# Padded k and q loads, zero-tile fillers, three more low parts over TensorE, and unpaced expert weight loads

## The chip, the cores and the metric

The kernel runs on one core of one Trainium2 chip. The metric is device time in microseconds. Five engines run their own instruction queues in order: TensorE (matmuls), VectorE, ScalarE, GpSimd (POOL) and SyncE (SP, which here only issues loads). Data moves by 16 DMA engines. Profiles call VectorE DVE and ScalarE ACT; PEld is TensorE's weight load.

## The reference

Three stages are computed one after the other, on 4 sequences of 768 tokens with 8 heads of 48:

```python
# 1. gated linear attention, per head
state = alpha[t][:, None] * state + outer(k[t], v[t]);  y[t] = q[t] @ state
# 2. a dense layer, x: (3072, 384)
h = x @ w_in                                 # (384, 2048)
x = maximum(0.01 * h, h) @ w_out             # (2048, 384)
# 3. eight experts, each token to its best one
e = argmax(x @ w_gate); p = softmax(x @ w_gate)[e]
out = p * (maximum(x @ w1[e], 0) @ w2[e])    # w1[e]: (384, 1024), w2[e]: (1024, 384)
```

The dense layer's w_in and w_out arrive as 64-bit floats. The kernel takes their bits apart on VectorE and represents each scaled weight by two float16 parts, a high one (hi) and what is left (lo); products are summed as hi*hi + hi*lo + lo*hi.

## The kernel before, in words

Tokens are worked on in eight units of 384 (`NU`, `UT`). For each unit, alpha, k, q and v are loaded, VectorE forms running decays from alpha by a scan (L584), ScalarE their logarithms and inverses (L587, L589), and four VectorE products (L624) scale k and q by them into kt and qt. TensorE then transposes kt (L647), forms scores (L718), states and outputs (L679, L752, L759) in three chunks of 128 tokens, and the outputs are scaled (xh, L772), transposed and split into two float16 parts (L780 to L794). That is xT, the input of the dense layer, `moe1` (first half L830, second half L839; the leaky step in between is L807 to L814 on ScalarE, VectorE and POOL). After a unit, `finish` and `route` choose each token's expert and scatter its row to a table in HBM (L974).

Ahead of and beside the first unit the dense weights are unpacked. `w_in_piece` handles w_in in 12 pieces of 128 x 512: three VectorE passes over the bits (L421, L423, L425), the high part on ScalarE (L444), and then the low part in one of two ways: for pieces 0 to 5 two TensorE products that subtract the high part (L451, L452) and a ScalarE cast (L454), for pieces 6 to 11 one VectorE pass (L447). `w_out_piece` does the same bit passes for 16 pieces; `logit_weights` transposes each (L484), copies it out of PSUM scaled on ScalarE or VectorE, whichever the planner finds free (L488, L490), and multiplies it with w_gate (L495).

k and q come as two loads of 48 partitions each, into partitions 0 to 47 and 64 to 111 of a tile whose other partitions were set to zero once (L317 on POOL, L319 on ScalarE).

The order of all engines' queues is written by a planner, `Loom`, when the program is built. It keeps a clock for each engine, takes the chain of steps that could start first, and among those that could start within 0.25 us of it the one with the lowest priority number. A step names its cost (`O("A", 0.65)`), the events it needs and posts, and the ring buffers it takes. Load steps (`"D"`) have costs of their own, and a posted event of a load counts as landed some microseconds later. Where the planner sees TensorE idle for more than 0.5 us in the first two units, it puts filler matmuls there (`keep_warm`, L396), as many as the gap divided by 0.24; their operand is the float16 identity, made by POOL (L322).

The third stage runs over 26 tiles of 128 places in the table, in four phases of 256 columns of the experts' inner dimension. `first_weights` loads and splits phase 0's weights in 16 loads of 384 KB (`first_piece`: squares on ScalarE L357, the high part on ScalarE or VectorE, the low part on VectorE L1189), while the dense layer still runs, three buffers in a ring. When they and the dense layer's first half are done, the second phase's 16 loads may begin (`second_weights`); what is left of them is spread over the tiles of phase 0. Each tile stages its expert's weights two tiles ahead (`stage`, L1257), and TensorE does L1340 (first product) and L1369 (second). The rows of a tile are gathered (L1204) and transposed (L1218) some tiles ahead. `last_tiles` carries the last unit's routing and the second part of the table in between.

## Time and profile before

| | us |
|---|---|
| median of 3 runs | 785.34 (784.45 to 787.21) |
| the profiled execution | 784.73 |
| its span | 783.0 |
| TensorE busy | 748.6 (96%) |
| VectorE busy | 611.0 (78%) |
| ScalarE busy | 483.4 (62%) |
| POOL busy | 374.4 (48%) |

The span is what the profile covers; the execution's own time is 1.7 us more. Busy is the time in which an instruction of the engine runs; a matmul's end is modelled, so TensorE's share is not its share of peak. In rows of the timeline an `xN` is N instructions merged, and the bracket at the end is the idle time before the first of them and what ended it. [...]

### The profile page before, as it was taken

Reading aid. Unit: us, or ns where it says so; the run is one execution under the profiler, and the core shown is the slowest. Engines: PE = TensorE matmul, PEld = TensorE weight load, DVE = VectorE, ACT = ScalarE, POOL = GpSimd, SP = SyncE. Lnnn points to the kernel's source line nnn. Section 1 sums busy time; section 2 is a strip of 40 time slices with the busy share of each in tenths; the row PEclk is TensorE's granted clock in tenths of the full one; section 3 lists DMA queues with packets and bytes.
Section 4 is the critical chain, followed back from the end, with each engine's and each line's share of the span. In section 5 each row is a group of like instructions: output and inputs, shape, how many; then the busy total and the mean of one; then the engine's idle time right before and its main releaser. Section 6 shows DMA issues by size and latency. Waiting matters only on the chain.

```text
span 783.0 us, 20274 instructions
## 1 busy us (share of the span) xinstructions
PE 748.6 (96%) x7554; PEld 513.6 (66%) x7554; DVE 611.0 (78%) x1442; ACT 483.4 (62%) x1080; POOL 374.4 (48%) x406
## 2 busy tenths in 40 slices
PE   6989998999999999999999999998989999999994
PEld 2746665666566666766766665656877777777773
DVE  7899998489879868967965466574878899999664
ACT  5667654689976765774675382545666666667530
POOL 9126114523563272463373062363452487886543
PEclk9999999999999999999999999999999999999998
DMA  9663541154534535523001203115378565654342
GB/s 288 209 181 102 183 104 54 55 127 132 152 107 125 146 92 129 139 58 101 3 11 42 82 32 117 48 42 171 112 258 269 163 203 148 218 164 143 127 166 79
DMA packets 52872, 99.47 MB, mean 127 GB/s; under 512 B 5149, under 2 KB 37971, under 8 KB 52768
## 3 DMA queue, kind: packets, MB, share of 16 engines
q1 hardware_dynamic: 39104, 70.89, 31.8%
q0 software_dynamic: 4960, 14.62, 5.4%
q10 hardware_dynamic: 8704, 12.58, 4.6%
q8 instruction: 64, 1.05, 0.6%
q14 instruction: 40, 0.33, 0.1%
HBM read 76.03 MB, written 9.86 MB: 110 GB/s over the span
## 4 chain that ended last, share of the span: by engine, by line
PE 74%; DMA 7%; DVE 6%; POOL 5%; issue 4%; ACT 3%; DVEq 0%; ACTq 0%; POOLq 0%; SPq 0%
PE m L830 22%; PE m L839 20%; PE a L1340 9%; PE m L1369 9%; DMA wr<-in_moe_w 4%; PE a L718 3%; PE m L396 2%; POOL W L1140 2%; PE a L759 2%; PE a L679 1%; PE a L746 1%; PE a L647 1%; DMA so<-W 1%; DMA al<-in_aT 1%; PE a L495 1%
## 5 line engine op out<-in xcount | busy, mean ns | idle before, releaser
L839 PE MATMUL m<-woh,gh 128*128 128x392 f16 x1152 | 201.9, 330 | 0.0
L830 PE MATMUL m<-xT,wih 128*128 128x384 f16 x1152 | 194.0, 326 | 4.0 <-ACT xT L791 1.7
L814 POOL TENSOR_TENSOR gh<-gf,gh 128x384 f16<-128x384 f32 x128 | 118.8, 939 | 159.3 <-ACT gh L812 155.5
L830 PEld LDWEIGHTS <-wih 128*128 128x128 f16 x1152 | 111.4, 98 | 77.3 <-issue 4.7
L839 PEld LDWEIGHTS <-gh 128*128 128x128 f16 x1152 | 110.1, 98 | 73.4 <-issue 0.4
L1340 PE MATMUL a<-XT,st 128*128 128x128 f16 (+1 forms) x1872 | 116.8, 215 | 4.8 <-DVE st L1257 2.6
L1369 PE MATMUL m<-W,hs 128*128 (+1 forms) x624 | 119.3, 327 | 2.2 <-issue 1.6
L1340 PEld LDWEIGHTS <-st 128*128 128x128 f16 x1872 | 105.8, 98 | 22.6 <-DVE st L1257 4.7
L809 DVE SCALAR_TENSOR_TENSOR gf<-m,gf 128x384 f32<-128x384 f32 x128 | 70.2, 555 | 64.0 <-ACT gf L807 62.9
L1257 DVE COPY st<-W 128x1536 f16 x104 | 89.7, 863 | 22.2 <-PE m L1369 11.8
L807 ACT ACTIVATE gf<-m 128x384 f32<-128x384 f32 x128 | 62.4, 489 | 53.1 <-PE m L830 51.5
L1348 ACT ACTIVATE hs<-a 128x256 f16<-128x256 f32 x104 | 39.5, 381 | 68.1 <-PE a L1340 43.7
L1369 PEld LDWEIGHTS <-hs 128*128 128x128 f16 (+1 forms) x720 | 57.6, 101 | 31.9 <-issue 3.7
L812 ACT CAST gh<-gf 128x384 f16<-128x384 f32 x128 | 64.3, 506 | 11.3 <-DVE gf L809 11.2
L1140 POOL TENSOR_TENSOR W<-wr,W 128x768 f16<-128x768 f32 x32 | 56.8, 1777 | 4.5 <-ACT W L1139 4.4
L1204 POOL DMA_INDIRECT acc<-x_rows,offj x26 | 31.2, 1198 | 37.5 <-DVE offj L1201 31.2
L1352 DVE SCALAR_TENSOR_TENSOR hs<-a,hs 128x256 f16<-128x256 f32 x104 | 43.1, 414 | 7.2 <-ACT hs L1348 4.9
L1113 POOL TENSOR_SCALAR wr<-wr 128x768 f32<-128x768 f32 x32 | 29.8, 931 | 31.0 <-DMA wr<-in_moe_w 16.6
L357 ACT ACTIVATE scrap<-W 128x768 bf16<-128x768 f16 x48 | 40.2, 838 | 5.6 <-ACT hs L1348 3.9
L1390 POOL DMA_INDIRECT out<-acc x26 | 26.6, 1023 | 31.9 <-DVE acc L1387 20.9
L885 DVE TENSOR_REDUCE mx<-m 128x1 f32<-128x384 f32 x24 | 13.3, 553 | 33.8 <-PE m L839 28.9
L974 POOL DMA_INDIRECT x_rows<-xg,pi x24 | 25.0, 1041 | 23.0 <-PE m L830 5.2
(282 smaller groups left out, 1253.1 us busy)
## 6 DMA issues: line engine op xcount, KB each, us to landing
wr<-in_moe_w SPq DMA_DIRECT2D x64, 384.0 KB
so<-W ACTq DMA_DIRECT2D x32, 384.0 KB
al<-in_aT SPq DMA_DIRECT2D x16, 390.0 KB
raw_in<-in_moe_w_in SPq DMA_DIRECT2D x12, 512.0 KB
raw<-in_moe_w_out SPq DMA_DIRECT2D x16, 384.0 KB
ck<-in_moe_w_in SPq DMA_DIRECT2D x24, 256.0 KB
ck<-in_moe_w_out SPq DMA_DIRECT2D x32, 192.0 KB
kn__125<-in_kT SPq DMA_DIRECT2D x16, 288.0 KB
```

The costliest lines, as they stand in the source:

```text
L357: A.activation(scrap, src, AF.Square, scale=scale, accum_out=g_sq[:, i : i + 1])
L807: A.activation(gf, ph[:, 0:UT], AF.Copy, scale=0.01 * CG)
L809: V.scalar_tensor_tensor(gf, ph[:, 0:UT], CG, gf, ALU.mult, ALU.max)
L812: A.copy(gh[:, 0], gf)
L814: E_[e].tensor_tensor(out=gh[:, 1], in0=gf, in1=gh[:, 0], op=ALU.subtract)
L830: T.matmul(ph[:, 0:UT], wih[:, a, kk, f * P : (f + 1) * P], xT[:, b, kk, :], start=(n == 0), stop=(n == 8),)
L839: T.matmul(po[:, 0:ROW], g[f][:, a, c * P : (c + 1) * P], woh_[0][:, b, f, :], start=(n == 0), stop=(n == 3 * NF - 1),)
L1140: G.tensor_tensor(out=lo, in0=raw, in1=hi, op=ALU.subtract)
L1257: V.tensor_copy(out=sth[i % 2].rearrange("p a k f -> p a (k f)"), in_=Wp[ph][0][:, :, ds(reg(V, j), 1), :, :].rearrange("p a e k f -> p a ...
L1340: T.matmul(hp[:, f * P + z * w : f * P + (z + 1) * w], st[z][:, a, kk, f * P : (f + 1) * P], XT[j][:, b, kk, z * w : (z + 1) * w], start=( ...
L1352: V.scalar_tensor_tensor(hs[:, 1].rearrange("p i t -> p (i t)"), hp[:, 0 : 2 * P], 0.0, hs[:, 0].rearrange("p i t -> p (i t)"), ALU.max, A ...
L1369: T.matmul(yp[z * w : (z + 1) * w, 0:DM], hs[:, a, i, z * w : (z + 1) * w], w2, start=(n == 0), stop=(n == 5), skip_group_check=True,)
```

## The change

Five edits.

1. The fillers multiply a 128 x 128 float16 tile `idle` that VectorE sets to zero as its first instruction, instead of the identity. Their count is now (gap - 0.5)/0.25, and (gap - 2.0)/0.25 for the first gap.
2. The host pads k and q with zero rows to 64 per head, and one load of 128 partitions brings each; the tiles' zeroing goes. Their priority among the first unit's loads rises above that of the second w_in load. The planner's cost of loads in the first 20 us changes.
3. The low parts of w_in pieces 6, 7 and 8 go by TensorE and ScalarE as those of 0 to 5 do.
4. The scaled transposes of w_out are always copied by ScalarE.
5. The loads of the experts' first weights follow one another from issue to issue, not from landing to issue; pieces 11 to 15 get priority 1.5 instead of 20. The first two stages need the table only, and the last unit's three scatters go out in one step of `last_tiles`.

```diff
@@ Loom.do
-                self.warm(int((gap - 0.5) / 0.24))
+                self.warm(int((gap - (0.5 if self.clock["P"] else 2.0)) / 0.25))
...
-            t += us * (0.75 if e == "D" and t < DSTART else 1)
+            t += us * ((0.6 if t < 20 else 0.75) if e == "D" and t < DSTART else 1)
...
-        landed = t + op.lag + ((2.0 if t < DSTART else 4.0) if last == "D" else 0.0)
+        landed = t + op.lag + ((2.6 if t < 20 else 2.0 if t < DSTART else 4.0) if last == "D" else 0.0)
@@ tile_kernel
-    zero = cp.tile([P, 1], F32, name="zero")
-    V.memset(zero, 0.0)
+    idle = cp.tile([P, P], F16, name="idle")
+    V.memset(idle, 0.0)
...
-        t = pa.tile([P, 4, UT], F32, name=nm)
-        for p in (32, 96):
-            if nm == "kn_":
-                G.memset(t[p : p + 32], 0.0)
-            else:
-                A.copy(t[p : p + 32].rearrange("p a t -> p (a t)"), zero[p : p + 32].to_broadcast([32, 4 * UT]))
-        qk.append(t)
+        qk.append(pa.tile([P, 4, UT], F32, name=nm))
@@ keep_warm
-                    to.rearrange("p (a t) -> p a t", a=4), ident16,
-                    ident16.unsqueeze(1).to_broadcast([P, 4, P]), start=True, stop=True,
+                    to.rearrange("p (a t) -> p a t", a=4), idle,
+                    idle.unsqueeze(1).to_broadcast([P, 4, P]), start=True, stop=True,
@@ w_in_piece
-        if n >= 6:
+        if n >= 9:
@@ logit_weights
-        e = yield O("A", 0.5, take=[("wt", f)], free=[("a", ("wt", f))], alt=("V", (0.5,)))
+        yield O("A", 0.5, take=[("wt", f)], free=[("a", ("wt", f))])
...
@@ load_k
-        yield O("D", 2.6, take=[(nm, u, 2)], post=[(nm, u)])
-        for z in range(2):
-            nc.sync.dma_start(out=t[64 * z : 64 * z + D].rearrange("p a t -> p (a t)"), in_=src[u, z])
+        yield O("D", 3.1, take=[(nm, u, 2)], post=[(nm, u)])
+        nc.sync.dma_start(out=t.rearrange("p a t -> p (a t)"), in_=src[u])
@@ route
-            elif c:
-                yield
@@ first_weights
-            loom.add(first_piece(n, e, which), 20, now=loom.clock["V"])
+            loom.add(first_piece(n, e, which), 20 if n < 11 else 1.5, now=loom.clock["V"])
@@ first_piece
-        yield O("D", 1.8, take=[("wr", n)], need=[("wd", n - 1)] if n else (), post=[("wd", n)])
+        yield O("D", 1.8, take=[("wr", n)], need=[("wd", n - 1)] if n else ())
         raw = raw_weights(0, e, which)
+        loom.ev["wd", n] = loom.clock["D"], "D"
@@ first_stages
-            yield O("v", 0.75, need=[("wr", n) for n in range(E)] + [("acc", i)])
+            yield O("v", 0.75, need=[("wr", n) for n in range(E)] + ["table"])
@@ the units' loads
-            loom.add(load_k(u, nm, src, t), at - 0.7 * early)
+            loom.add(load_k(u, nm, src, t), at - 0.99 * early)
@@ last_tiles
         for _ in second_table():
-            next(work, None)
             yield
@@ _laid_out
+    def padded(a):
+        return np.pad(turned(a), ((0, 0), (0, 0), (0, 64 - D), (0, 0))).reshape(NU, P, H // 2 * UT)
...
-        "qT": turned(q),
-        "kT": turned(k),
+        "qT": padded(q),
+        "kT": padded(k),
```

## Rows read from the trace of the kernel before

**Rows 1.** Windows: start:end, length, five engines' busy us, PEclk, DMA share, GB/s.

```profile
0.00:21.00 21.00, 14.96 (x59) 6.40 (x60) 14.70 (x25) 10.00 (x15) 19.21 (x51) 1.00 0.91 279
21.00:40.00 19.00, 19.00 (x268) 13.90 (x267) 16.23 (x41) 13.44 (x28) 1.03 (x2) 1.00 0.67 218
21.00:54.00 33.00, 30.12 (x328) 19.82 (x327) 29.96 (x66) 21.88 (x44) 2.04 (x3) 1.00 0.74 225
54.00:100.00 46.00, 45.76 (x394) 29.13 (x394) 42.71 (x78) 31.63 (x84) 19.96 (x27) 1.00 0.42 130
100.00:136.00 36.00, 30.58 (x373) 22.18 (x373) 33.41 (x92) 18.66 (x46) 9.32 (x13) 0.95 0.30 69
136.00:517.00 381.00, 378.67 (x3213) 245.28 (x3211) 276.46 (x698) 253.63 (x591) 173.77 (x189) 1.00 0.32 89
517.00:545.00 28.00, 27.78 (x215) 17.87 (x214) 16.48 (x52) 11.58 (x20) 11.03 (x12) 1.00 0.36 107
570.00:606.00 36.00, 32.33 (x471) 25.41 (x469) 28.72 (x58) 25.25 (x42) 15.02 (x11) 1.00 0.87 282
```

**Rows 2.** TensorE's waits over the span: in total, times, longest.

```profile
PE m L396 <- POOL ident L322: 6.0, 1, 6.0
```

**Rows 3.** Timeline of the start and one later wait: start, length, instructions.

```profile
0.88 0.06 DVE L305 MEMSET zero<- 128x1 f32 x1 [0.88 <-PEq L1781]
6.04 15.06 PE L396 MATMUL m<-ident 128*128 128x512 f16 x58 [6.04 <-POOL ident L322]
11.01 9.60 PEld L396 LDWEIGHTS <-ident 128*128 128x128 f16 x45 [0.15 <-issue]
12.24 0.96 DVE L624 SCALAR_TENSOR_TENSOR kt<-kn__125,Ft 128x768 f32<-128x768 f32 x1 [1.18 <-POOL sm L343]
14.92 0.96 DVE L624 SCALAR_TENSOR_TENSOR qt<-qn__128,R 128x768 f32<-128x768 f32 x1 [0.75 <-DMA qn__128<-in_qT]
16.67 0.95 DVE L624 SCALAR_TENSOR_TENSOR qt<-qn__128,Ft 128x768 f32<-128x768 f32 x1
20.94 1.04 PE L647 MATMUL a<-ident,kt 128*128 128x128 f32 x8
23.16 0.74 DVE L720 COPY_PREDICATED sm<-tri,a 128x512 f32<-128x512 int32 x1 [3.37 <-PE a L718]
...
120.19 1.65 PE L780 MATMUL a<-ident,xh 128*128 128x128 f32 x6 [3.34 <-ACT xh L772]
```

**Rows 4.** Windows of the first loads: 48-row loads, then 128-row loads.

```profile
8.00:14.00 6.00, 6.00 (x22) 2.43 (x21) 4.79 (x8) 3.24 (x7) 5.80 (x18) 1.00 1.00 205
15.00:19.00 4.00, 4.00 (x21) 1.77 (x19) 4.00 (x6) 0.00 (x0) 3.53 (x9) 1.00 1.03 423
```

**Rows 5.** Lines (busy us, mean ns | idle before); L396 up to 60 us only.

```profile
L396 PE MATMUL m<-ident 128*128 128x512 f16 x65 | 16.9, 423 | 6.0 <-POOL ident L322 6.0
L451 PE MATMUL m<-w,ids 128*128 128x512 f32 x12 | 6.4, 619 | 0.0
L452 PE MATMUL m<-wih,idn 128*128 128x512 f16 x6 | 2.3, 380 | 0.0
L447 DVE SCALAR_TENSOR_TENSOR wih<-w,wih 128x512 f16<-128x512 f32 x6 | 4.1, 686 | 0.2 <-ACT wih L444 0.2
L490 DVE TENSOR_SCALAR wt<-a 128x384 f32<-128x384 f32 x4 | 2.2, 556 | 0.3 <-PE a L484 0.2
```

**Rows 6.** Timeline where the expert tiles begin.

```profile
545.26 0.96 DVE L1189 SCALAR_TENSOR_TENSOR W<-wr,W 128x768 f16<-128x768 f32 x1 [0.94 <-ACT W L1185]
546.74 0.56 DVE L1257 COPY st<-W 128x1536 f16 x1 [0.40 <-issue]
547.36 0.84 PE L1340 MATMUL a<-XT,st 128*128 128x128 f16 x12 [2.13 <-DVE st L1257]
```

**Rows 7.** The first weights' low parts (ns min/median/max, first and last start), and ScalarE's longest wait.

```profile
L1189 DVE SCALAR_TENSOR_TENSOR W<-wr,W x16: 942/951/2980, 438.5 to 545.3; 128x768 f16<-128x768 f32 x16
476.55 0.84 ACT L357 ACTIVATE W<-wr 128x768 bf16<-128x768 f32 x1 [5.76 <-DMA wr<-in_moe_w]
```

More of the change, by code (lines that the diff above doesn't have):

```diff
@@ L484, in logit_weights @@
             T.transpose(pt[:, kk * P : (kk + 1) * P], w32[:, kk * P : (kk + 1) * P], ident)
-        e = yield O("A", 0.5, take=[("wt", f)], free=[("a", ("wt", f))], alt=("V", (0.5,)))
+        yield O("A", 0.5, take=[("wt", f)], free=[("a", ("wt", f))])
         wt = tm.tile([P, DM], F32, tag="wt", name="wt", bufs=2)
-        if e == "A":
-            A.activation(wt, pt[:, 0:DM], AF.Copy, scale=SB)
-        else:
-            V.tensor_scalar(wt, pt[:, 0:DM], SB, None, ALU.mult)
+        A.activation(wt, pt[:, 0:DM], AF.Copy, scale=SB)
         yield O("P", 0.35, take=[("a", ("lg", f))], free=[("wt", f)])
```

## The prediction

> **What bounds the kernel now.** I read the stretches of the span first. From 136 to 517 us TensorE is busy 378.67 of 381 us and the granted clock is 1.00; 517 to 545 (27.78 of 28) looks the same [rows 1]. Nothing in the diff shortens that work, so the change can only act where TensorE has slack: 0 to 21, 21 to 54, 100 to 136, and from 545 to 606 us. The list of TensorE's waits is headed by 6.0 us on the float16 identity that POOL makes [rows 2]; the next is the 3.34 us on ScalarE's xh that ends at 120.19 [rows 3]. The start then needs the timeline. TensorE's 58 fillers run from 6.04 to 21.10, the first real matmul (the transposes of kt, L647) starts at 20.94, but its last input, the fourth product on VectorE (L624), ended at 16.67 + 0.95 = 17.62 [rows 3]. So 3.3 us of the start are fillers standing in front of work that was ready: the planner asked for 58, counted from 0, and they could begin only at 6.04. VectorE pays too: it idles 3.37 us before its first L720, waiting for TensorE [rows 3]. From 21 to 136 VectorE is the fuller engine beside TensorE: 29.96 of 33, 42.71 of 46, 33.41 of 36 us [rows 1]. It and TensorE share the bound there.
>
> **1. Fillers on a zeroed tile.** The tile is VectorE's first memset, so TensorE can start near 1.1 us instead of 6.04: VectorE's first memset ran from 0.88 to 0.94 [rows 3]. Of the 58 fillers, 13 took 11.01 - 6.04 = 4.97 us, at the lower clock for most of it, and 45 took 21.10 - 11.01 = 10.09 us, 0.224 each [rows 3]. The new count is (gap - 2.0)/0.25; following the planner's list by hand with its new costs I get a gap near 15.4, so 53 fillers: 1.1 + 4.97 + 40 x 0.224 = 15.0 us. Four fillers more or less move this by 0.9 us. The POOL and ScalarE steps that zeroed k's and q's spare rows go as well; they stood ahead of the identity, on which nothing in this stage then waits.
>
> **2. k and q whole.** Before, VectorE waited 1.18 us ahead of its first product, put down to a POOL memset that part 1 also moves forward, and 0.75 us ahead of its second, by name for q's load, until 14.92 [rows 3]. Two 48-row loads per tensor are replaced by one of 128 rows, 768 KB instead of 576. From 8 to 14 us, when mainly the 48-row loads move, the DMA engines are busy at 1.00 of their time and carry 205 GB/s; from 15 to 19 us, with 128-row loads of w_in and v, 423 GB/s at the same busy share [rows 4]. The rows don't say whether the slow packets are slow for their length (6144 bytes) or for the 48 partitions. With the length as cause, the two padded loads take 1536/205 = 7.5 us, with the partitions as cause 1536/423 = 3.6; the four halves took 1152/205 = 5.6. They are also issued one w_in load (512 KB, 1.2 us) earlier on SP. So q lands 5.6 + 1.2 - 3.6 = 3.2 us sooner, at 11.7, or 0.7 later, at 15.6. The w_in load they pass lands 1.2 us behind q, before the products end. I take the partitions: the rows at 423 are the same kind of load. [...] At 11.7 q is there before VectorE wants it (14.92 - 0.75 - 1.18 = 13.0), both waits go, and the products end at 17.62 - 1.93 = 15.7. At 15.6 the last three products, 0.875 us apart (14.92 to 16.67), end near 18.3. Since fillers end at 15.0, what is late next is VectorE: the transposes start near 15.75 instead of 20.94: **-5.2 us** (-2.6 at the slow end). Later units load 16 x 192 KB more; DMA is busy 0.30 to 0.42 of the time after 54 us [rows 1], so I cost that at nothing; were it uncovered it would be 3.1 MB/423 = 7 us.
>
> **3. Low parts of three more w_in pieces over TensorE.** For pieces 6 to 8 one VectorE pass of 0.686 us goes (4.1 us over six pieces: L447), 2.1 us in all, and L451, L452 and a ScalarE cast come, as for pieces 0 to 5, whose L451 and L452 were busy 6.4 + 2.3 us over six, 1.45 us per piece [rows 5]: 4.4 us on TensorE. Between 21 and 54 us TensorE has 33 - 30.12 = 2.9 us idle, and 7 fillers (65 up to 60 us less the 58; 16.9 - 15.06 = 1.8 us) [rows 1, 3, 5]. That is 4.7 us of slack, made by VectorE's lateness; the 4.4 fit into it if VectorE runs ahead. It does: its two waits and the 3.37 us idle go (5.3) and 2.1 us of its work, 7.4 in all against TensorE's 5.2. I put the stage at **-0.3 us** (bounds: +4.4 if nothing is absorbed, -2.2 if VectorE's 7.4 comes through).
>
> **4. Scaled transposes of w_out only on ScalarE.** Four passes of 0.556 us leave VectorE (L490) [rows 5], 2.2 us, and about as much lands on ScalarE, which is busy 31.63 of 46 us there [rows 1]. The gain shows only where VectorE sets the end, from 100 to 136: TensorE does 30.58 us of 36 there, fillers included, waits 3.3 us in one piece on ScalarE, and the granted clock is 0.95 [rows 1, 3]. I take **-1.5 us**: VectorE's lead of 2.2 from part 3 and the 2.2 here, of which ScalarE's in-order queue gives back most. Bounds: +2.2 (ScalarE in full) to -4.4.
>
> **5. Experts' first weights without pauses.** Each load was planned to wait for the landing of the one before; VectorE's 16 closing passes (L1189) stretch from 438.5 to 545.3 us, one per 7.1 us [rows 7]. The last one, at 545.26, held up the staging copy L1257 at 546.74 and with it TensorE for 2.13 us [rows 6]. With pauses gone and the last five at a nearer priority, the sixteen end well before; the 2.1 us go. Then the second set (16 loads) may begin while the first layer still ends, at 517, instead of inside the expert tiles. From 570 to 606 us those loads and the copies of split tiles fill DMA to 0.87 and TensorE is idle 3.7 us [rows 1]. If half the second set has moved forward, half of that goes: 1.8, rounded down for what the forwarded loads cost the gathers, 1.3. **-3.4 us** in all (bounds 0 and -5.8; the loss side is rival E). The last unit's three scatters now go out in one step: on POOL two come up to two tiles sooner, in front of gathers that are planned four tiles ahead, so at nothing; uncovered, 2 us. Stages that need the table instead of the gathered rows only move within VectorE's queue.
>
> **Sum.** -5.2 - 0.3 - 1.5 - 3.4 = -10.4. The profiled execution took 784.73 us (span 783.0), so 774.3; the median of the runs, 785.34, is 0.6 above it: **775 us**.
>
> **Rivals.**
> B, the weights give nothing: the second set still starts inside the expert tiles, and some other pass holds up the third stage. Only the first three terms remain, -7.0: 778. For it: TensorE's order is fixed by a planner, and each plan leaves its own gaps.
> C, VectorE's lead comes through whole: -7.4 - 2.2 up to 136 and -5.8 after: 785.3 - 15.4 = 770.
> D, the extra f32 passes come in full: from 21 to 40 us TensorE is busy 19 of 19 us [rows 1], so pieces planned there are added: -5.2 + 4.4, nothing else gained: 784.5. Against it: pieces 6 to 8 belong to the third quarter of w_in, which is worked on later, where the slack is.
> E, slower: without the landing in its sum, the planner puts ScalarE's squares (L357) ahead of the data; ScalarE then stands with the first layer's evictions queued behind it. One such block of 5.76 us, to 476.55, lies in a stretch where TensorE lost 2.3 of 381 us in all [rows 1, 7]. It decides from the point where blocks last longer than that: if eleven of the sixteen last 1 us more, 11 us are lost against the 7.0 kept: 789. Against it: loads run up to three ahead, so most have landed.
> F, the change doesn't do what it says: zeros don't raise the clock. Then the first 4.97 us after the fillers run at the lower clock and half of that, 2.5 us, is given back: 777.5.
>
> **How the numbers follow.** Forecast 0.48, B 0.22, C 0.11, D 0.10, E 0.06, F 0.03. A measurement of this kernel can't tell less than 0.3% (2.4 us) from no change, so faster means under 783.0 and slower over 787.7. D is the same, E slower, and 0.02 of B and the forecast's own spread falls into the same: 0.82, 0.12, 0.06. The range reaches from just under C to over B's spread, short of D: 769 to 782; left out are E, D and a little below C, about 0.2.
>
> **What would show it.** Right: fillers from about 1.1 to 15 us, L647 at 15.5 to 16.5; no VectorE idle at its first L720; 6144-byte loads above 350 GB/s; nine L451 pieces, and the dense L830 run some 5 us sooner; no L490; the sixteen L1189 ended before 530; no 2 us wait at the third expert tile; less TensorE idle in the following 60 us. Wrong: L647 later than 17.5, TensorE's gap at the change of units (100 to 136) as long as before, ScalarE waits on wr that end in TensorE idle between 420 and 545. The prediction falls if the stretch before the 136 us mark gains under 4 us.

## The result, and the profile after

The changed kernel takes **775.21 us** (median of 4 runs, 773.22 to 777.18) where the kernel before takes 785.99 in the same comparison: a ratio of 0.9864, 95% interval 0.9829 to 0.9899, or 7.9 to 13.4 us less. The forecast was 775. The sum was right; the runs below show that its terms were not, and that the errors cancelled, which was luck: the start brought more than its term up to the end of the dense layer, and by itself lost more than half of that again behind it. The profiled execution took 773.22 us (span 771.5), 11.51 less than that of before.

Helper lines have moved: fillers are now L390, the k transposes L637, the scores L708, the products L614, the dense layer L820 and L829, the expert products L1329 and L1358.

The stretches of the changed kernel (windows; columns as in [rows 1], PEclk the granted TensorE clock as a share of full speed; its record begins 7.1 us into this span, 10.9 us into that of before, and ahead of that it reads 1.00), cut at the corresponding points of its work:

```profile
0.00:16.00 16.00, 14.94 (x58) 6.18 (x60) 12.97 (x23) 7.07 (x13) 14.39 (x44) 1.00 0.89 342
16.00:49.00 33.00, 32.08 (x336) 21.17 (x335) 32.42 (x69) 25.46 (x54) 6.51 (x10) 1.00 0.70 273
...
94.00:131.00 37.00, 36.71 (x415) 25.23 (x413) 29.29 (x73) 25.03 (x58) 10.92 (x13) 1.00 0.30 96
131.00:505.00 374.00, 370.08 (x3140) 239.99 (x3138) 281.09 (x709) 251.38 (x581) 174.72 (x185) 0.99 0.31 97
505.00:535.00 30.00, 30.00 (x227) 19.23 (x224) 17.73 (x58) 8.87 (x16) 13.71 (x16) 1.00 0.38 113
...
560.00:596.00 36.00, 32.51 (x476) 25.83 (x474) 28.00 (x58) 24.96 (x43) 13.31 (x10) 1.00 0.85 271
```

Against [rows 1]: the gap before the second unit is nearly gone (36.71 of 37 us busy where 30.58 of 36 stood). The long middle, which I had taken as fixed, got worse: 3.9 us without a matmul where 2.3 stood, and a mean granted clock of 0.99. The 36 us after the first expert tiles are as before, 3.5 us idle.

The start (timeline of TensorE and VectorE), to be held against [rows 3]:

```profile
1.06 14.77 PE L390 MATMUL m<-idle 128*128 128x512 f16 x54 [1.06 <-DVE idle L305]
8.97 0.96 DVE L614 SCALAR_TENSOR_TENSOR kt<-kn__125,Ft 128x768 f32<-128x768 f32 x1
11.62 0.95 DVE L614 SCALAR_TENSOR_TENSOR qt<-qn__126,R 128x768 f32<-128x768 f32 x1
14.24 0.94 DVE L614 SCALAR_TENSOR_TENSOR kt<-kn__125,R 128x768 f32<-128x768 f32 x1
15.77 1.16 PE L708 MATMUL a<-qt,kt 48*128 48x128 f32 x16
17.29 0.73 DVE L710 COPY_PREDICATED sm<-tri,a 128x512 f32<-128x512 int32 x1
```

No product waits for k or q (no bracket), the last of the four ends at 14.24 + 0.94 = 15.18, the fillers at 1.06 + 14.77 = 15.83, the first real matmul starts at 15.77, and VectorE no longer idles before its first masked copy.

The groups by line (busy us, mean ns, idle before) of the fillers (66 in the whole span, 54 of them at the start) and the w_in pieces, against [rows 5]:

```profile
L390 PE MATMUL m<-idle 128*128 128x512 f16 x66 | 17.9, 433 | 1.1 <-DVE idle L305 1.1
...
L445 PE MATMUL m<-w,ids 128*128 128x512 f32 x18 | 9.5, 610 | 0.0
L446 PE MATMUL m<-wih,idn 128*128 128x512 f16 x9 | 3.4, 379 | 0.0
...
L441 DVE SCALAR_TENSOR_TENSOR wih<-w,wih 128x512 f16<-128x512 f32 x3 | 2.1, 684 | 0.0
```

The extra passes cost 9.5 + 3.4 - 6.4 - 2.3 = 4.2 us of TensorE.

New is a pair of gaps at the change to the third unit, 3.1 us idle in all. The timeline of TensorE there, and the window around it:

```profile
183.12 0.67 PE L669 MATMUL a<-vt,kn 128*64 128x48 f32 x16 [1.54 <-issue]
...
185.47 2.08 PE L708 MATMUL a<-qt,kt 48*128 48x128 f32 x16 [1.19 <-DVE qt L614]
```

```profile
180.00:190.00 10.00, 7.27 (x56) 5.05 (x55) 9.73 (x28) 8.52 (x21) 2.70 (x2) 0.73 0.66 236
```

VectorE is the full engine in these 10 us (9.73), and the second gap is TensorE's wait for its product of q; the first has no releaser in the profile. The clock's record reads half from 184.5 for 6.8 us.

Where the expert tiles begin: the low parts of the first weights (ns min/median/max, first and last start), and TensorE's waits from 530 to 605 us, against [rows 6, 7]:

```profile
L1178 DVE SCALAR_TENSOR_TENSOR W<-wr,W x16: 944/958/1589, 436.1 to 518.2; 128x768 f16<-128x768 f32 x16
```

```profile
PE a L1329 <- ACT XT L1209: 2.0, 3, 1.4
...
PE a L1329 <- DVE st L1246: 0.8, 1, 0.8
```

The sixteen end 27 us sooner, and the 2.13 us wait for the staging copy is 0.8. Of the second set's 16 loads 5 are now issued before the loads pause (the fifth at 530.1, the next at 558.4), where before the change it was 3 (the third at 546.2, the next at 570.6).

**Where the time went.** I split TensorE's time at the start of the last matmul of the dense layer, which stands behind all of that layer's work. "Other work" is the time in which a matmul other than a filler ran (where two overlap, the time counts for the one that started first); stretches at half clock lengthen it (in the changed kernel nine matmuls of L820 took 3.06 us from 187.48, at half, and 1.64 from 191.47, at full). The last column leaves out the 7 to 9 us after the last matmul. All of it is added up from TensorE's rows of one profile per kernel; the rows in bold are the two kernels of the case, and two programs were profiled twice, which shows how far such numbers repeat. The rows with a star are from a chip on which the last quarter of the expert stage took 1 to 5 us less than on the others (last section), so their last two columns are to be compared among themselves.

| kernel | edits in it | layer ends | idle | fillers | other work | from there to the end | idle in that |
|---|---|---|---|---|---|---|---|
| **before** | none | 541.8 | 16.9 | 21.3 | 503.6 | 241.2 | 9.9 |
| **after** | 1 2 3 4 5 | 532.5 | 7.1 | 17.4 | 508.1 | 239.0 | 8.1 |
| after, again | 1 2 3 4 5 | 532.0 | 8.0 | 16.7 | 507.3 | 238.4 | 7.8 |
| start alone | 1 2 | 530.6 | 7.6 | 22.2 | 500.9 | 248.3 | 13.5 |
| no 3, no 5* | 1 2 4 | 529.9 | 7.5 | 21.9 | 500.4 | 246.0 | 13.3 |
| six pieces | 1 2 4 5 | 530.5 | 7.5 | 22.5 | 500.5 | 238.9 | 8.2 |
| paced weights | 1 2 3 4 | 528.6 | 6.8 | 17.0 | 504.9 | 242.4 | 11.0 |
| without 4 | 1 2 3 5 | 533.9 | 8.0 | 20.7 | 505.2 | 240.7 | 8.3 |
| old fillers | 2 3 4 5 | 535.3 | 9.2 | 19.1 | 507.0 | 238.8 | 7.5 |
| 48-row loads | 1 3 4 5 | 532.7 | 11.1 | 17.4 | 504.3 | 242.1 | 11.2 |
| two 64-row loads* | 1 to 5 | 537.0 | 12.8 | 16.9 | 507.3 | 235.4 | 5.7 |
| fillers to unit 3* | 1 to 5 | 530.4 | 6.2 | 18.6 | 505.7 | 233.4 | 3.7 |
| the same, again | 1 to 5 | 530.9 | 6.8 | 18.6 | 505.6 | 239.2 | 8.2 |
| replanned* | 1 to 5 | 533.8 | 12.1 | 15.5 | 506.2 | 237.2 | 5.4 |

From before to after: idle -9.8, fillers -3.9, other work +4.5 up to the layer's end, and -2.2 behind it.

### The profile page after: what moved, and what is told of

Its sections match the earlier page's. It is cut to its first block, busy times and chain, and to the rows that moved or that the text cites. A ratio compares the mean times of both kernels' runs of the same rounds, so it can differ in the third digit from the quotient of the medians.

```text
span 771.5 us, 20245 instructions
## 1 busy us (share of the span) xinstructions
PE 749.0 (97%) x7543; PEld 513.6 (67%) x7543; DVE 604.0 (78%) x1435; ACT 481.5 (62%) x1083; POOL 377.9 (49%) x406
## 4 chain that ended last, share of the span: by engine, by line
PE 84%; DVE 8%; DMA 3%; ACT 2%; issue 1%; ACTq 0%; POOL 0%; DVEq 0%; POOLq 0%; SPq 0%
PE m L829 22%; PE m L820 21%; PE a L1329 13%; PE m L1358 12%; PE a L708 3%; PE m L390 2%; PE a L749 2%; DMA wr<-in_moe_w 2%; DMA so<-W 2%; PE a L669 1%; PE a L736 1%; PE a L637 1%; PE a L1207 1%; PE a L486 1%; DVE w L417 1%
## 5 line engine op out<-in xcount | busy, mean ns | idle before, releaser
L829 PE MATMUL m<-woh,gh 128*128 128x392 f16 x1152 | 201.7, 329 | 0.0
L820 PE MATMUL m<-xT,wih 128*128 128x384 f16 x1152 | 195.2, 328 | 1.0 <-DVE gf L799 1.0
L820 PEld LDWEIGHTS <-wih 128*128 128x128 f16 x1152 | 112.2, 99 | 75.0 <-issue 3.7
L829 PEld LDWEIGHTS <-gh 128*128 128x128 f16 x1152 | 110.3, 98 | 73.0
L1358 PE MATMUL m<-W,hs 128*128 (+1 forms) x624 | 119.7, 326 | 2.8 <-ACT hs L1337 1.3
L1329 PE MATMUL a<-XT,st 128*128 128x128 f16 (+1 forms) x1872 | 116.8, 215 | 3.2 <-ACT XT L1209 2.0
L1329 PEld LDWEIGHTS <-st 128*128 128x128 f16 x1872 | 106.0, 98 | 20.7 <-issue 4.5
L1246 DVE COPY st<-W 128x1536 f16 x104 | 80.9, 778 | 24.9 <-PE a L1329 14.9
L1358 PEld LDWEIGHTS <-hs 128*128 128x128 f16 (+1 forms) x720 | 57.9, 101 | 32.8 <-issue 3.6
L1341 DVE SCALAR_TENSOR_TENSOR hs<-a,hs 128x256 f16<-128x256 f32 x104 | 43.2, 415 | 11.8 <-ACT hs L1337 11.2
L723 POOL TENSOR_TENSOR sh<-sm,sh 128x512 f16<-128x512 f32 x17 | 23.6, 1395 | 27.3 <-ACT sh L718 27.2
```

The source lines that it names most:

```text
L820: T.matmul(ph[:, 0:UT], wih[:, a, kk, f * P : (f + 1) * P], xT[:, b, kk, :], start=(n == 0), stop=(n == 8),)
L829: T.matmul(po[:, 0:ROW], g[f][:, a, c * P : (c + 1) * P], woh_[0][:, b, f, :], start=(n == 0), stop=(n == 3 * NF - 1),)
L1246: V.tensor_copy(out=sth[i % 2].rearrange("p a k f -> p a (k f)"), in_=Wp[ph][0][:, :, ds(reg(V, j), 1), :, :].rearrange("p a e k f -> p a ...
L1329: T.matmul(hp[:, f * P + z * w : f * P + (z + 1) * w], st[z][:, a, kk, f * P : (f + 1) * P], XT[j][:, b, kk, z * w : (z + 1) * w], start=( ...
L1341: V.scalar_tensor_tensor(hs[:, 1].rearrange("p i t -> p (i t)"), hp[:, 0 : 2 * P], 0.0, hs[:, 0].rearrange("p i t -> p (i t)"), ALU.max, A ...
L1358: T.matmul(yp[z * w : (z + 1) * w, 0:DM], hs[:, a, i, z * w : (z + 1) * w], w2, start=(n == 0), stop=(n == 5), skip_group_check=True,)
```

## The experiments

They ran in three groups, each on one chip with the kernel before beside it: its median was 786.46 us in the first (old fillers, 48-row loads, six pieces, paced weights), 782.05 in the second (two 64-row loads, fillers to the third unit, no 3 and no 5, replanned) and 785.92 in the third (the rest). Ratios are to it.

**Old fillers: edit 1 undone.**

```diff
-                self.warm(int((gap - (0.5 if self.clock["P"] else 2.0)) / 0.25))
+                self.warm(int((gap - 0.5) / 0.24))
...
-                    to.rearrange("p (a t) -> p a t", a=4), idle,
+                    to.rearrange("p (a t) -> p a t", a=4), ident16,
```

> The changed kernel with edit 1 undone: fillers multiply the float16 identity again and are counted by (gap - 0.5)/0.24. Mine: in the changed kernel POOL's identity cast ends at 1.73 us, since the zeroing in front of it is gone, so fillers start near 1.8 and not at 6.04; some 62 of them end near 17.7 and the first real matmul starts there instead of 15.77, about 2 us late. Part of that is taken up again where TensorE has slack (118 and 182 us): 775 to 777. Rival (the tile alone made the 5 us): first real matmul at 20 or later, 779 to 780. Rival (every new plan of the queues moves the end by some us, whatever the edit): anything from 770 to 782, with the first matmul no guide to it.

777.42 us (775.10 to 779.45), a little over my 775 to 777; ratio 0.9890 [0.9852, 0.9929]. The timeline of its start:

```profile
1.79 16.51 PE L388 MATMUL m<-ident 128*128 128x512 f16 x62 [1.79 <-POOL ident L314]
18.23 0.94 PE L706 MATMUL a<-qt,kt 48*128 48x128 f32 x12
```

With nothing to zero ahead of it the identity is there at 1.79 instead of 6.04, but 62 fillers are asked for and stand before the first real matmul until 18.23, 2.5 us later than in the changed kernel. The delay stays: against the profile above it is 2.5 us at the second unit, 2.8 at the layer's end and 2.6 at the end of the span; against the changed kernel's second profile (below) it is 2.0, 3.3 and 3.7.

**48-row loads: edit 2 undone.**

```diff
-        yield O("D", 3.1, take=[(nm, u, 2)], post=[(nm, u)])
-        nc.sync.dma_start(out=t.rearrange("p a t -> p (a t)"), in_=src[u])
+        yield O("D", 2.6, take=[(nm, u, 2)], post=[(nm, u)])
+        for z in range(2):
+            nc.sync.dma_start(out=t[64 * z : 64 * z + D].rearrange("p a t -> p (a t)"), in_=src[u, z])
```

(The zeroing, the unpadded k and q and the planner's old costs and priority for these loads come back with it, so the order of the queues is another, too.)

> The changed kernel with edit 2 undone: k and q in two loads of 48 rows each, their spare rows zeroed on POOL and ScalarE, the loads' old costs and priority. Mine: 6144-byte rows carry 163 to 180 GB/s again, VectorE waits 1 to 2 us before its first products, the first real matmul comes at 17.5 to 18 (fillers end before), 2 us late; TensorE's gap at the change to unit 1 stays closed, since these loads come long before they are needed there: 776 to 778. Rival (the quicker loads closed the gap at 116 to 121 us): that gap opens again, 782 to 785.

779.69 us (776.52 to 784.06), between my 776 to 778 and the rival's 782 to 785; ratio 0.9929 [0.9904, 0.9953]: by the medians the dearest of the five to take away. Timeline of the start, and TensorE's waits before the second unit (95 to 131 us):

```profile
15.06 0.99 DVE L623 SCALAR_TENSOR_TENSOR qt<-qn__130,R 128x768 f32<-128x768 f32 x1 [1.12 <-DMA qn__130<-in_qT]
...
17.07 1.06 PE L646 MATMUL a<-ident,kt 128*128 128x128 f32 x8 [3.02 <-POOL place__109 L376]
```

```profile
PE a L779 <- ACT xh L771: 2.3, 2, 1.3
```

VectorE waits for q again, and the first real matmul comes 1.3 us later. (The profile puts its wait down to POOL's L376, which ended at 16.97; the matmul's input, VectorE's third product, had ended at 16.92.) The idle before the second unit is 6.4 us in place of 1.7: I had expected that gap to stay closed. The late start alone doesn't open it so far: with the old fillers TensorE starts 2.5 us late and the gap stays at 1.8, and in the next run, where the order is kept, VectorE's last product is 4.2 us late and the gap is 3.5. How much of the rest is the other order wasn't tried.

**Two 64-row loads.** The same padded bytes in rows of 6144, but each tensor in two loads of 64 partitions.

```diff
-        nc.sync.dma_start(out=t.rearrange("p a t -> p (a t)"), in_=src[u])
+        for z in range(2):
+            nc.sync.dma_start(
+                out=t[64 * z : 64 * z + 64].rearrange("p a t -> p (a t)"), in_=src[u, 64 * z : 64 * z + 64]
+            )
```

> The changed kernel, every queue's order kept, but each padded k and q tile comes in two loads of 64 rows (0 to 63, 64 to 127): same bytes, same 6144-byte rows, two issues on SP. Mine (the 48-row loads were slow for the partitions that one load covers): 6144-byte packets take about 450 ns again instead of 234, the windows of these loads carry about 200 GB/s, q lands some 4 us later, the first real matmul comes at 16.5 to 18.5. TensorE's gap at the change to unit 1 (1.74 us idle in all from unit 0 to unit 1) stays closed, because the order is the same and these loads come long before their use there: median 775.5 to 778. Rival (the rows' length, or the count of loads): rate as in the changed kernel, first matmul at 15.8, 775. Rival (the quicker loads themselves closed the gap, as the run with 48-row loads would have it with 6.4 us idle): 4 us or more idle there, 780.

774.94 us (773.72 to 776.47), ratio 0.9915 [0.9888, 0.9943]. One window of 8 to 14 us, first of the changed kernel, then of this one, and this one's product of q:

```profile
8.00:14.00 6.00, 6.00 (x30) 2.70 (x29) 5.92 (x9) 3.11 (x7) 5.64 (x16) 1.00 1.01 416
```

```profile
8.00:14.00 6.00, 6.00 (x30) 2.70 (x28) 3.23 (x6) 3.32 (x7) 5.34 (x24) 1.00 1.01 223
```

```profile
15.79 0.96 DVE L617 SCALAR_TENSOR_TENSOR qt<-qn__126,R 128x768 f32<-128x768 f32 x1 [0.97 <-DMA qn__126<-in_qT]
```

DMA is busy all the time in both, and carries 416 or 223 GB/s. The median packet of 6144 bytes takes 234 ns with one load of 128 partitions, 440 with two of 64, 465 in the kernel before with 48. The length of the rows is the same in all three, and the size of a load isn't the cause either: a 384 KB load of w_out to 128 partitions, as large as one of 64 rows, moves a 3072-byte packet in 121 ns in this run. It is the partitions of one load: 440 ns with 64 against 234 with 128. The first real matmul is at 19.42, later than the 16.5 to 18.5 I had expected, and idle to the layer's end is 12.8 us where the changed kernel has 7.1. The gap before the second unit, which I had expected to stay closed, is 3.5.

**Six pieces: edit 3 undone.**

```diff
-        if n >= 9:
+        if n >= 6:
```

> The changed kernel with edit 3 undone: pieces 6 to 8 of w_in get their low parts on VectorE again (2.1 us more there, 4.4 us less on TensorE). Mine (VectorE's lead closed the gap at the change to unit 1): unit 1's dense run starts 2 to 3 us later relative to the first matmul, 776 to 778. Rival (the f32 passes are a cost that TensorE carries): 771 to 773. Rival (plans differ, no size): gap opens or not without relation to 2.1 us.

773.12 us (771.35 to 774.21), ratio 0.9835 [0.9807, 0.9863]. The fillers' group by line, and the window of the change to the third unit:

```profile
L390 PE MATMUL m<-idle 128*128 128x512 f16 x93 | 23.8, 406 | 1.1 <-DVE idle L305 1.1
```

```profile
180.00:190.00 10.00, 10.00 (x134) 7.34 (x133) 9.86 (x22) 8.36 (x21) 5.25 (x4) 1.00 0.34 113
```

The float32 passes are replaced by fillers almost one for one: 22.5 us of fillers up to the layer's end in place of 17.4, and 7.6 less other work, the 4.2 of the passes and 3.4 that are left, half of the 6.8 us at half clock. The gap before the second unit is longer (4.2 us idle), as I had expected, but that at the third unit and the half clock are gone, and the layer ends 2.0 us sooner. My 776 to 778 missed. Edit 3 gives nothing that shows, and by the medians it may cost 2 us; the intervals of the two ratios overlap, so that is not shown.

**Paced weights: edit 5 undone.**

```diff
-        yield O("D", 1.8, take=[("wr", n)], need=[("wd", n - 1)] if n else ())
+        yield O("D", 1.8, take=[("wr", n)], need=[("wd", n - 1)] if n else (), post=[("wd", n)])
...
-            loom.add(first_piece(n, e, which), 20 if n < 11 else 1.5, now=loom.clock["V"])
+            loom.add(first_piece(n, e, which), 20, now=loom.clock["V"])
```

(And the stages' condition, and the three scatters in a step each, as before.)

> The changed kernel with edit 5 undone: loads of the experts' first weights wait for one another's landing, all at priority 20, stages wait for the gathered rows, scatters in three steps. Mine: the last low part falls into the first expert tiles again and TensorE waits 1.5 to 2.2 us for the third tile's stage, nothing else: 776.5 to 777.5, all of the difference between 500 and 560 us, none before. Rival (the second set of loads moved forward matters as well): 3 to 5 us, also from 560 to 600. Rival (nothing): 775.

773.20 us (772.41 to 777.87), ratio 0.9850 [0.9807, 0.9892]. TensorE's waits of 520 to 606 us:

```profile
PE a L1330 <- DVE st L1247: 1.9, 1, 1.9
PE a L1208 <- DMA acc<-x_rows,offj: 1.6, 2, 1.1
```

The staging wait is back, as expected, and what follows the layer takes 242.4 us in place of 239.0; but the layer ends 3.9 us sooner, and the time is under my 776.5 to 777.5. About 3.2 of the 3.9 is other work: this profile has the two gaps at the third unit (3.1 us idle), but no half clock behind them. That need not be the edit's doing: two profiles of the changed kernel differ there as well (below).

**No 3 and no 5.** The two edits above together, taken back:

```diff
-        if n >= 9:
+        if n >= 6:
...
-        yield O("D", 1.8, take=[("wr", n)], need=[("wd", n - 1)] if n else ())
+        yield O("D", 1.8, take=[("wr", n)], need=[("wd", n - 1)] if n else (), post=[("wd", n)])
```

> Edits 1, 2 and 4 alone (3 and 5 undone). Mine: edit 3 adds 4.4 us of TensorE's work and takes away 7 us of fillers and 2.5 of idle time ahead of unit 1, of which most is given back by unit 3, so its sum is about +2; edit 5 is within 1 to 2 us of nothing: 771 to 774. Rival (the two parts add up as measured alone, -2 and -2): 771. Rival (the plan moves by itself): up to 778.

777.65 us (772.57 to 779.83), where I had expected 771 to 774; ratio 0.9937 [0.9908, 0.9965], clear of six pieces, from which it differs by edit 5 alone. Its waits of 520 to 606 us:

```profile
PE a L1208 <- DMA acc<-x_rows,offj: 9.6, 2, 6.3
```

The staging copy is not the wait here; the gathers are. So edit 5 is worth 0.010 of the time, some 8 us, in one plan (order of the queues) and nothing that shows in another.

**Start alone: edits 1 and 2 on the kernel before**, whose code for the other three stands:

```diff
-        if n >= 9:
+        if n >= 6:
...
-        yield O("A", 0.5, take=[("wt", f)], free=[("a", ("wt", f))])
+        e = yield O("A", 0.5, take=[("wt", f)], free=[("a", ("wt", f))], alt=("V", (0.5,)))
...
-        for _ in second_table():
-            yield
+        for _ in second_table():
+            next(work, None)
+            yield
```

> Edits 1 and 2 alone on the kernel before. By my prediction this is worth -5.2 us: a ratio of 0.9934, first real matmul near 15.8, the dense run of the first unit some 5 us sooner, and the gap of 8.3 us before the second unit's as long as before. Rival (the runs so far): the earlier start also closes part of that gap, down to 4 to 5 us idle, and the second unit's dense run comes 8 to 9 us sooner; then some of it must be given back later for the total to stay near -5 to -7.

781.77 us (780.66 to 785.14), ratio 0.9953 [0.9931, 0.9974], as the rival had it: the gap before the second unit is half closed (4.1 us of 8.3), and part of the gain is given back later. The first real matmul is at 16.52. The dense layer ends at 530.6, 11.2 us sooner than before, sooner even than with all five edits. Then 7.1 us are lost behind it: 3.6 of idle, and the record of the clock reads half for 6.8 us from 558.8. TensorE's waits of 530 to 605 us, its timeline at the longest, and POOL's at the same place:

```profile
PE a L1211 <- DMA acc<-x_rows,offj: 6.2, 2, 4.8
```

```profile
561.34 0.82 PE L1211 MATMUL a<-ident,acc 128*128 128x128 f16 x6 [4.80 <-DMA acc<-x_rows,offj]
```

```profile
545.57 1.15 POOL L967 DMA_INDIRECT x_rows<-xg,pi  x1 [3.02 <-DVE xg L964]
550.30 1.01 POOL L1197 DMA_INDIRECT acc<-x_rows,offj  x1 [3.58 <-DVE XT L1064]
...
554.32 1.20 POOL L967 DMA_INDIRECT x_rows<-xg,pi  x1 [2.80 <-ACT acc L1373]
558.12 1.03 POOL L1197 DMA_INDIRECT acc<-x_rows,offj  x1 [2.61 <-DVE hs L1345]
...
562.10 1.03 POOL L967 DMA_INDIRECT x_rows<-xg,pi  x1 [2.76 <-DMA acc<-x_rows,offj]
565.79 1.03 POOL L1197 DMA_INDIRECT acc<-x_rows,offj  x1 [2.67 <-DMA x_rows<-xg,pi]
```

The gather that ended the wait is, by its time, the one issued at 558.12. It stands on POOL behind a scatter of the last unit at 554.32, 8.7 us after the scatter before it. Scatters (L967) and gathers (L1197) alternate here, and at each change of kind POOL idles 2.6 to 3.6 us. The same place in the changed kernel:

```profile
548.11 1.32 POOL L962 DMA_INDIRECT x_rows<-xg,pi  x1 [2.99 <-DVE tnt L1035]
...
549.91 1.00 POOL L962 DMA_INDIRECT x_rows<-xg,pi  x1 [0.28 <-DVE tdu L1045]
...
551.40 0.98 POOL L962 DMA_INDIRECT x_rows<-xg,pi  x1 [0.28 <-issue]
554.99 1.06 POOL L1193 DMA_INDIRECT acc<-x_rows,offj  x1 [2.61 <-DVE tlm L1068]
```

Three scatters in 4.3 us, 0.28 us of idle between them, then the gathers, and TensorE waits for none of them. Scatters in three steps don't always alternate with gathers; with paced weights they don't:

```profile
542.38 1.01 POOL L1194 DMA_INDIRECT acc<-x_rows,offj  x1 [1.71 <-DVE offj L1191]
...
546.55 1.05 POOL L964 DMA_INDIRECT x_rows<-xg,pi  x1 [2.96 <-DVE con L1030]
...
548.26 1.12 POOL L964 DMA_INDIRECT x_rows<-xg,pi  x1 [0.45 <-POOL xg L963]
...
551.27 0.98 POOL L964 DMA_INDIRECT x_rows<-xg,pi  x1 [1.70 <-DVE hs L1342]
```

The gathers issued before the first of these scatters tell the cases apart. The first part of the table has 14. In the kernel before and with paced weights all 14 have gone, and the three scatters follow one another. With start alone and with no 3 and no 5 only 12 have, and the last two come between the scatters. In the ten profiles with the scatters in one step 12 or 13 have gone, and no gather comes between; TensorE's longest total wait for gathers in these ten is 2.6 us (48-row loads), against 6.2 and 9.6. So among the parts of edit 5 it is the one step that fits all fourteen profiles; it was not tried alone.

**Without 4.**

```diff
-        yield O("A", 0.5, take=[("wt", f)], free=[("a", ("wt", f))])
+        e = yield O("A", 0.5, take=[("wt", f)], free=[("a", ("wt", f))], alt=("V", (0.5,)))
```

> Edit 4 is undone: a scaled transpose of w_out may again go to VectorE or ScalarE. My step in the prediction put edit 4 at -1.5 us, so this kernel should be 1 to 2 us slower than the changed one on this chip, with the gap of TensorE between the first dense L820 run of the first unit and that of the second some 1.5 us longer than 1.74. Rival: what closed that gap is the plan as a whole, and any edit undone reopens it by 2 us or more (48-row loads gave 6.44, six pieces 4.24); then idle of 3.5 us or more stands there and the time is 2 to 5 us longer. Second rival: the change in the gap is given back at the change to the third unit, as with six pieces, and the time is the same within 1 us.

776.73 us (776.28 to 778.11), ratio 0.9893 [0.9849, 0.9937]; the changed kernel beside it took 774.69 (772.12 to 775.66). So 2.0 us by the medians, about what the prediction gave edit 4, although the profile shows the larger effect that the rival named: TensorE idles 4.9 us before the second unit, not 1.7, and part is given back at the third.

**The changed kernel again, and with fillers through the third unit.** The second asks for fillers one unit longer; six more are placed.

```diff
-            if u == 1:
+            if u == 2:
                 loom.warm = None
```

> The changed kernel as it is, on the same chip as the next three, so that they can be compared with it directly. Expected: a ratio to the kernel before of 0.985 to 0.990, and TensorE's wait of about 1.2 us on the product of q and the decays at 181 to 188 us again, since the program and its order are the same; the half clock behind that gap may be there or not (the one profile so far had 6.8 us of it). If the gap is missing, it belonged to that one execution and my account of what was given back falls.

> The changed kernel, with fillers allowed through the third unit: exactly six more fillers, where TensorE idles near 182 us, and no other instruction moved. Mine: the gap is not shorter, but the granted clock stays at 1.00 there, and the 2 to 3 us that the half clock of 6.8 us cost in the changed kernel's profile are kept in every execution: 773 and a narrower spread. Rival (the dip costs nothing or comes seldom): 775.

> The kernel with fillers through the third unit again, now on the same chip as the changed kernel itself. If its earlier gain is real it is 1.5 to 4 us under the changed one here, all of it gained between 181 and 265 us (the wait at the change to the third unit shorter, no half clock). If only the chip made the difference (the earlier chip ran the kernel before 4.4 us faster than the chips of the first runs), the two are equal within 1 us.

The changed kernel: 774.69 us, ratio 0.9866 [0.9823, 0.9909], with the same two gaps and 3.4 us of half clock behind them instead of 6.8. Its first real matmul:

```profile
15.74 1.16 PE L708 MATMUL a<-qt,kt 48*128 48x128 f32 x16 [0.60 <-DVE kt L614]
```

With the fillers: 768.61, ratio 0.9842 [0.9808, 0.9875], and beside the changed kernel 773.85 (771.79 to 775.78), ratio 0.9859 [0.9810, 0.9908]. TensorE's timeline at the third unit in the latter of these two:

```profile
183.33 0.67 PE L669 MATMUL a<-vt,kn 128*64 128x48 f32 x16 [1.32 <-issue]
...
184.32 1.24 PE L390 MATMUL m<-idle 128*128 128x512 f16 x5
185.68 1.16 PE L708 MATMUL a<-qt,kt 48*128 48x128 f32 x16
```

Five of the fillers stand where the 1.19 us wait was, the clock stays at 1.00, and the fourth to eighth units start 1.6 to 1.7 us sooner than in the run beside it. Behind them 0.6 us is lost again up to the layer's end, so the two medians are 0.8 us apart with overlapping ranges. The good absolute time of the earlier run went with its chip, on which the kernel before was faster as well (782.05). No version tried is shown to beat the changed kernel.

**Replanned: EPS from 0.25 to 0.3**, the planner's tie width; no instruction is added by hand.

```diff
-EPS = 0.25
+EPS = 0.3
```

> The changed kernel with nothing changed but the planner's slack EPS, 0.30 instead of 0.25 us: the same work in another order. Rival that the order alone decides: the start as in the changed kernel, and the median up to 6 us away from 775, the gaps at the changes of unit at other places. Mine: some of that is so, the sum of idle time from 40 to 200 us stays at 5 to 8 us, and the median within 3 us.

771.62 us (769.04 to 778.65), ratio 0.9883 [0.9819, 0.9946]. Idle to the layer's end is 12.1 us instead of 7.1 and fillers are 1.9 us fewer; the second unit starts 3.5 us later and the ratio's interval overlaps that of the changed kernel. A shuffled order moves single gaps by as much as edits 3, 4 and 5 do.

## Why the prediction was right, point by point

**Fillers and whole loads, -5.2: right for the place, too small for the kernel.** The first real matmul came at 15.77 against the 15.75 of the sum, and that closely by luck: the sum had the fillers done at 15.0 and VectorE's products last, at 15.7; in this profile the products were done at 15.18, and the last fillers stood in front until 15.8. In the second profile of the same program VectorE was last, by 0.60 us. 54 fillers ran where 53 were reckoned; 14 of them 0.43 us apart before they run 0.22 apart (11 in the second profile, 12 before the change, 14 with the old fillers). The record of the clock begins where the spacing halves, at 7.1 us (10.9 before the change), and reads full from there; that the clock was lower ahead of it is my reading of the spacing. The spacing halves with a zero operand as with the identity, and rival F fell. Whether VectorE's first wait had been for the POOL memset that the prediction names is doubtful: with 48-row loads a wait of 0.98 us at the same place is put down to k's load. q was there when VectorE wanted it at 11.62; the choice of partitions over row length was right, as the 64-row loads show (440 ns a packet against 234, in rows of the same length). One sign I named for it was wrong: the padded loads don't run above 350 GB/s by themselves (317 for the first pair, from 5.5 to 10.5 us), since a w_in load shares the engines with them, which carry 379 together in that time. What I missed is the rest of the stage. I let VectorE's lead count for 0.3 + 1.5 us and booked that under edits 3 and 4. The kernel with edits 1 and 2 alone ends the layer 11.2 us sooner, of which 4.4 are the start (16.52 against 20.94).

**Low parts over TensorE, -0.3: nothing shown, a cost of 2 us not excluded.** That the 4.2 us would be absorbed was right: they took the place of fillers. But edits 3 and 4 only moved a gap. Edits 1 and 2 leave 4.1 us idle before the second unit (8.3 before the change), and about as much is left with 3 added (4.9, without 4) or with 4 added (4.2 with six pieces, 4.5 with no 3 and no 5); with both it is 1.7, and 3.1 us of idle at the third unit appear only then, in some executions with 6.8 or 3.4 us at half clock behind them, which I estimate to cost half of that, 3.4 or 1.7 us more.

**Scaled transposes, -1.5: 2.0 by the medians**, within an interval that holds nothing too.

**Unpaced weights, -3.4: the wait went, the rest did not.** Of the 2.1 us, 1.3 went; the 1.3 us from 570 to 606 did not come (3.5 us idle after, 3.7 before), for the second set hardly moved: 5 of its 16 loads were issued ahead of the pause where 3 had been, and the term supposed that half move forward. After the first three, each load is issued within 0.1 us of the end of a closing pass that frees one of the ring's three buffers, and the second set's own passes end at 528.5, 530.0 and then from 558.4 on. Measured against the kernel before, the span behind the layer is 2.2 us shorter. With edits 1, 2 and 4 alone TensorE waits 9.6 us for gathers, and edit 5 takes that away; with the other four in place there was 1.6 us to take, and undoing edit 5 costs nothing that shows. That wait was 0.2 us in the kernel before and in none of my rivals; I had the scatters "at nothing; uncovered, 2 us", and looked only at what their one step could cost. That the layer ends sooner is not enough to bring the wait: with paced weights it ends at 528.6, with start alone at 530.6. Of the kernels profiled it came in the two where the scatters went out in three steps and the first part's gathers were not all out when they began.

**136 to 517 us unchanged: wrong.** It lost 1.6 us more than before to gaps, and some to the clock. I read "busy 378.67 of 381" as a property of the stretch; it was one of that order of the queues.

So -10.4 came true as -11.5 between the profiles, in other parts. Taken in the order of start alone and then the rest, edits 1 and 2 give 4.1 us of it (11.2 up to the layer's end, 7.1 lost behind it) against the 5.2 of the sum, and the three others 7.4 against 5.2: they end the layer 1.9 us later and what follows 9.3 us faster, 7.1 of which is what edits 1 and 2 had lost there. Undoing one edit at a time moves the ratio from 0.9865 by +0.0025 (1), +0.0064 (2), -0.0030 (3), +0.0028 (4) and -0.0015 (5), which adds to 0.0072, about half of the 0.0135 of all five: the terms don't add, and only edit 2's stands outside the changed kernel's interval. Rivals B and D fell by their times, 778 and 784.5. B's mechanism did not fall: that the weights give nothing is what the run with paced weights shows for this kernel, within its interval. C was right that the lead comes through up to the layer's end, and wrong that as much again follows behind it. E did not come, as ScalarE's waits from 420 to 540 us show (total, times, longest), against [rows 7]:

```profile
ACT W L351 <- DMA wr<-in_moe_w: 5.8, 8, 1.3
```

Left open: what moves the gap from the second to the third unit, and whether the scatters' one step alone, without the rest of edit 5, would keep the gathers early.

## What to carry to other kernels

Gains before the bounding stretch are to be followed to a mark behind which the same work remains (here the last dense matmul), and split there into idle, fillers and other work; marks inside a planned order move with the order. What lies behind the gain can change with the new order, here the turn of scatters and gathers on POOL, so each such neighbour needs a price in the new order, not in the old. Undo edits in groups as well as singly: what was worth some 8 us without its neighbour (edit 5 without edit 3) showed no worth with it.

## What the runs showed of the hardware

- One load to all 128 partitions moves a 6144-byte packet in 234 ns (median), two of 64 partitions in 440, 48-row loads in 465; with a third more bytes the first k and q pair came in 5.0 us instead of 7.2.
- The same program with fillers through the third unit had a span of 763.8 us on one chip and 770.1 on another: 1.9 us of the difference up to the start of the experts' second phase, 4.5 in their fourth. From the first product of the fourth phase to the end of the span, all four kernels profiled on the first of these chips took 63.2 to 65.2 us, the ten other profiles show 66.5 to 68.6. Why was not tried.
- Behind the two gaps of 1.5 and 1.2 us at the third unit the record of the clock read half for 6.8 us in one execution and for 3.4 in another of the same program; of three other kernels with the same 3.1 us of idle there, one read half for 3.4 us (old fillers) and two read full (paced weights, two 64-row loads). With fillers in the second gap it read full in both profiles.
- Where an indirect scatter and an indirect gather on the same table followed one another on POOL, POOL idled 2.6 to 3.6 us between them (start alone; 2.7 to 3.4 up to 560 us with no 3 and no 5), between two scatters in one step 0.28 us (the changed kernel).
